# Attention gradients: accumulating dV and dK transposed, with 512-column moving operands and a crossbar turn of the result

## The chip, the cores and the metric

The kernel runs on one core of a Trainium2 chip. The metric is the device time of one execution in microseconds (us), the median of several. All runs quoted here were classed as fast runs: the granted TensorE clock was 0.994 to 0.998 of full speed in the profiled ones. Kernels are compared only within the same rounds. Engines are named PE (TensorE), PEld (its weight loads), DVE (VectorE), ACT (ScalarE), POOL (GpSimd) and SP (SyncE, which only issues DMAs here).

## The reference, cut to what matters

The reference computes a residual block (attention over a given K and V, times a gated MLP) and all its gradients. Only the attention and its gradients matter here; they take about 3.1 of the 5.0 ms. There are 32 heads, 2048 queries, 2048 keys and a head size of 128.

```python
q = (x @ wq).reshape(B, Sq, H, Dh)            # H = 32, Dh = 128, Sq = Sk = 2048
scores = einsum("bhqd,bhkd->bhqk", q, k_cache) * Dh ** -0.5
p = softmax(scores)
o = einsum("bhqk,bhkd->bhqd", p, v_cache)
# ... and by jax.vjp:   dV = P^T dO,   dP = dO V^T,   dS = P * (dP - delta),
#                       dK = dS^T Q,   dQ = dS K
```

## The kernel before: the parts that the change and the argument touch

A head takes 32 slots. In the first 16 ("pass 1") each slot makes one slab P of 128 queries x 2048 keys; in the next 16 ("pass 2") each turns one P slab into a dS slab in place. Each finished slab is turned by the DMA crossbar (issued by SP), and five slots later (`skew`) PE multiplies the turned slab (PT or dST) by V or K to get the output and dQ. PE's order is fixed in the program: if a turned slab has not landed by its slot, PE stands.

```python
            wpt = pool("wpt", 7 if fast else 4)      # turned slabs in flight
            skew = min(SKEW if fast else 2, NT // 2) # SKEW = 5
            def transpose_slab(hs, qt, name):
                T = wpt.tile([P, NT, P], bf, name=name, tag="PT")
                nc.sync.dma_start_transpose(T[:], hs.slabs[qt][:])   # 128 x 2048, 512 KB
                return T
            def tail_part(hs, T, rhs, part):         # uses the turned slab, L677
                ...
                for kt in range(part * NT // 2, (part + 1) * NT // 2):
                    nc.tensor.matmul(hs.acc[:, 0, :], lhsT=T[:, kt, :], rhs=rhs[:, kt, :], ...)
```

dV and dK are sums over the 16 slabs of a pass. They are taken in two halves of eight slabs (the first half is parked in SBUF as f32), a step of eight matmuls at a time, in between the rest. Before the change the *slab* is the stationary operand, so every 128x128 block of it is loaded as weights for one matmul of 128 columns:

```python
            class Partial:
                def step(self):
                    kt = self.kt
                    j = kt % 4
                    if j == 0:
                        self.tile = acc_tile()
                    for qt in range(self.lo, self.hi):
                        nc.tensor.matmul(self.tile[:, j, :], lhsT=self.slabs[qt][:, kt * P:(kt + 1) * P], rhs=self.rhs[:, qt, :], ...)   # L737
                    ...
                            fo_ = stg.tile([P, 4, P], bf, name="kvo", bufs=4)
                            nc.vector.scalar_tensor_tensor(fo_[...], self.tile[...], self.factor, self.part[...], ...)
                            nc.gpsimd.dma_start(self.out_dram...[:, k0:kt + 1, :], fo_[:, :j + 1, :])   # 128 KB
```

In the last head, SP also loads the first two blocks of the attention output, turned (`load_oT`, 1 MB each, into the buffers KQ and xnT), for the output projection that follows, and POOL loads rows of `wo`.

## Time and profile before

| | before |
|---|---|
| median (4 runs of the comparison) | 5018.9 us |
| attention, from the first dO^T matmul to the last head's | 3014.9 us, 31 heads |
| one head (distance of the heads' first dO^T matmuls) | 97.37 us, in 28 of 30 full heads to within 0.01 us |
| last head, to the first matmul of the output projection | 121.2 us |
| output projection | 148.4 us |
| all that follows | 1256.1 us |

The stretches are read from the starts of the first matmuls of each kind in the trace. These are lines of the page of the kernel before: busy time by engine, the digits of PE and its clock over 40 slices, DMA queues (packets, MB, share of 16 engines) and the costliest groups (busy us, mean ns of one, idle time before them).

```profile
PE 4914.6 (98%) x53584; PEld 3475.1 (69%) x54480; DVE 2582.2 (51%) x6721; ACT 2575.9 (51%) x4637; POOL 961.8 (19%) x1507
PE   9999999999999999999999999999889999999999
PEclk9999999999999999999999999999999999999999
...
q1 hardware_dynamic: 2659746, 699.38, 75.7%
q8 instruction: 428, 7.01, 0.6%
...
L737 PEld LDWEIGHTS <-Pq 128*128 128x128 bf16 x16384 | 1003.9, 98 | 244.3 <-issue 1.1
...
L737 PE MATMUL acc<-dOn,Pq 128*128 128x128 bf16 x8192 | 552.3, 219 | 10.1
L737 PE MATMUL acc<-Qn,Pq 128*128 128x128 bf16 x8192 | 540.6, 219 | 3.4
```

PE is the bound. A matmul's duration (219 ns) says little, because matmuls overlap; what counts is the distance of starts. The timeline of the kernel before shows it (start us, duration us, engine, line, operation, count):

```profile
1507.17 0.59 PE L700 MATMUL dp<-VT,dOT 128*128 128x512 bf16 x2
1507.60 1.06 PE L677 MATMUL acc<-Vn,PT 128*128 128x128 bf16 x16
1508.49 0.59 PE L700 MATMUL dp<-VT,dOT 128*128 128x512 bf16 x2
1508.92 1.06 PE L737 MATMUL acc<-dOn,Pq 128*128 128x128 bf16 x16
```

Two matmuls of 512 columns occupy 0.43 us (215 ns each) and sixteen of 128 columns 0.89 us (56 ns each): four narrow ones cost 224 ns where one wide one costs 216. The Trainium skill, page "TensorE: Matmul & The Clock Gate", section "Back-to-back issue gap", gives N/2.4 + 2.5 ns for N columns, and this trace agrees. The list of waits of PE in the 30 full heads has a single entry, so nothing else that the list shows delays PE there:

```profile
engine line waited for: us in total, times, longest us
PE acc L677 <- DMA dST<-Pq: 1.0, 1, 1.0
```

### The profile page before, as it was taken

To read this page: it belongs to the slowest core of one execution; us is meant where nothing else is said; L and a number is where in the kernel's file an instruction comes from. 1 tells how busy PE (TensorE), PEld (TensorE's weight loads), DVE (VectorE), ACT (ScalarE), POOL (GpSimd) and SP (SyncE) were. 2 spreads that over 40 slices of the span, in tenths; PEclk is the share of its full clock that TensorE was granted. 3 is DMA by queue.
4 is the path that set the end of the run, shared out by engine and by line. 5 is a ranking of instruction groups with operands and counts; after the bars stand their busy time and mean duration, and the time that the engine had idled before them with its cause. 6 is when DMAs were issued, how large, how long until landed. Compare 5 with 4: busy or idle time off the path is not lost.

```text
span 5024.2 us, 128236 instructions
## 1 busy us (share of the span) xinstructions
PE 4914.6 (98%) x53584; PEld 3475.1 (69%) x54480; DVE 2582.2 (51%) x6721; ACT 2575.9 (51%) x4637; POOL 961.8 (19%) x1507
## 2 busy tenths in 40 slices
PE   9999999999999999999999999999889999999999
PEld 4445787787787788778778877877646666555554
DVE  4545666666666666666666666665425444200111
ACT  5422766766666676666667666666413333211000
POOL 3322111111111111111111111111222222211000
PEclk9999999999999999999999999999999999999999
DMA  7887999999999999999999999999996665797876
GB/s 260 273 206 167 211 213 205 206 215 212 202 214 216 201 212 208 214 208 209 215 202 213 206 213 210 209 215 203 209 196 206 195 189 183 223 264 178 171 140 121
DMA packets 2762803, 1031.39 MB, mean 205 GB/s; under 512 B 2665377, under 2 KB 2669602, under 8 KB 2762210
## 3 DMA queue, kind: packets, MB, share of 16 engines
q1 hardware_dynamic: 2659746, 699.38, 75.7%
q0 software_dynamic: 101856, 323.05, 20.0%
q8 instruction: 428, 7.01, 0.6%
q14 instruction: 165, 1.35, 0.1%
q10 hardware_dynamic: 608, 0.59, 0.0%
HBM read 175.31 MB, written 182.13 MB: 71 GB/s over the span
## 4 chain that ended last, share of the span: by engine, by line
PE 92%; DMA 3%; issue 3%; DVE 1%; ACT 0%; SPq 0%; POOL 0%; POOLq 0%; ACTq 0%; DVEq 0%
PE acc L737 18%; PE acc L677 18%; PE acc L975 13%; PE sp L630 8%; PE dp L700 7%; PE acc L1157 6%; PE acc L213 6%; PE u_ps L448 3%; PE g_ps L446 3%; PE dh L1036 3%; PE acc L531 3%; PE acct L146 2%; PE acc L945 2%; DMA dST<-Pq 1%; DMA xnT<-on_d 1%
## 5 line engine op out<-in xcount | busy, mean ns | idle before, releaser
L648 ACT ACTIVATE Pq<-sp 128x1024 bf16<-128x1024 f32 x1024 | 1048.1, 1024 | 309.7 <-PE sp L630 196.4
L737 PEld LDWEIGHTS <-Pq 128*128 128x128 bf16 x16384 | 1003.9, 98 | 244.3 <-issue 1.1
L703 DVE SCALAR_TENSOR_TENSOR Pq<-dp,negdelta,Pq 128x1024 bf16<-128x1024 f32 x512 | 655.3, 1280 | 37.7 <-PE acc L677 36.5
L706 ACT ACTIVATE t<-dp,negdelta 128x1024 bf16<-128x1024 f32 x512 | 568.1, 1116 | 178.4 <-PE dp L700 123.0
L677 PEld LDWEIGHTS <-PT 128*128 128x128 bf16 x8192 | 501.0, 98 | 128.6 <-DMA PT<-Pq 11.5
L677 PE MATMUL acc<-Vn,PT 128*128 128x128 bf16 x8192 | 547.4, 219 | 17.0 <-DMA PT<-Pq 10.1
L737 PE MATMUL acc<-dOn,Pq 128*128 128x128 bf16 x8192 | 552.3, 219 | 10.1
L677 PE MATMUL acc<-Kn,dST 128*128 128x128 bf16 x8192 | 551.3, 219 | 9.1 <-DMA dST<-Pq 5.5
L630 PE MATMUL sp<-KQ 128*128 128x512 bf16 x1762 | 547.1, 379 | 2.2 <-ACT Pq L648 2.1
L737 PE MATMUL acc<-Qn,Pq 128*128 128x128 bf16 x8192 | 540.6, 219 | 3.4
L700 PE MATMUL dp<-VT,dOT 128*128 128x512 bf16 x1728 | 540.8, 379 | 0.0
L707 DVE TENSOR_TENSOR Pq<-t,Pq 128x1024 bf16<-128x1024 bf16 x512 | 354.6, 693 | 359.7 <-ACT t L706 351.9
L677 PEld LDWEIGHTS <-dST 128*128 128x128 bf16 x8192 | 492.0, 98 | 68.2 <-DMA dST<-Pq 7.4
L718 ACT ACTIVATE dq_n<-acc,rsc 128x128 bf16<-128x128 f32 x512 | 188.4, 368 | 331.7 <-PE acc L677 329.4
L1174 DVE SCALAR_TENSOR_TENSOR junk<-acc,xn_all 128x512 f32<-128x512 f32 (+1 forms) x32 | 13.9, 453 | 635.6 <-ACT dxn L1173 635.6
L751 POOL DMA_DIRECT2D out_dram<-kvo x256 | 140.8, 550 | 999.7 <-DVE kvo L749 999.7
L671 POOL DMA_DIRECT2D on_d<-o_n x128 | 97.3, 760 | 721.4 <-DVE junk L689 374.8
L1038 DVE TENSOR_TENSOR du_blk<-dh,ah 128x256 bf16<-128x256 f32 x288 | 120.4, 419 | 195.5 <-PE dh L1036 193.4
L1173 ACT ACTIVATE dxn<-acc 128x512 f32<-128x512 f32 (+1 forms) x32 | 12.8, 407 | 396.7 <-PE acc L1157 389.2
L635 DVE TENSOR_REDUCE rs_all<-rsp 128x1 f32<-128x2 f32 x512 | 78.1, 153 | 255.7 <-ACT Pq L648 253.4
L50 DVE TENSOR_SCALAR o_n<-acc,rinv_all 128x128 bf16<-128x128 f32 x352 | 123.3, 350 | 161.5 <-PE acc L677 161.5
L648 ACT ACTIVATION_READ_ACCUMULATOR Pq<-sp 128x1 f32 x1024 | 200.5, 196 | 0.0
(213 smaller groups left out, 6977.0 us busy)
## 6 DMA issues: line engine op xcount, KB each, us to landing
out_dram<-kvo POOLq DMA_DIRECT2D x256, 128.0 KB, 4.2
ah<-a_d POOLq DMA_DIRECT2D x18, 1024.0 KB, 7.2
ah<-h_d POOLq DMA_DIRECT2D x18, 1024.0 KB, 9.4
du_d<-du_blk POOLq DMA_DIRECT2D x18, 1024.0 KB, 8.0
dg_d<-dg_blk POOLq DMA_DIRECT2D x18, 1024.0 KB, 9.7
h_d<-h_row POOLq DMA_DIRECT2D x64, 256.0 KB, 3.5
a_d<-a_row POOLq DMA_DIRECT2D x64, 256.0 KB, 3.7
x_all<-in_A_k_cache_dram SPq DMA_DIRECT2D x64, 256.0 KB, 3.8
```

The costliest lines, as they stand in the source:

```text
L213: nc.tensor.matmul(av[:, :CH], lhsT=w[:, i, :], rhs=srcT[:, i, cs], start=(i == 0), stop=(i == DT - 1))
L630: nc.tensor.matmul(sp[:, c * CH:(c + 1) * CH], lhsT=hs.QT[:, qt * P:(qt + 1) * P], rhs=hs.KT[:, hf * HW_ + c * CH: hf * HW_ + (c + 1) * CH ...
L648: nc.scalar.activation(Pq[:, hsl], sp[:], AF.Exp, scale=SCALE, accum_out=hs.rsp[:, hf:hf + 1])
L677: nc.tensor.matmul(hs.acc[:, 0, :], lhsT=T[:, kt, :], rhs=rhs[:, kt, :], start=(kt == 0), stop=(kt == NT - 1))
L700: nc.tensor.matmul(dp[:, c * CH:(c + 1) * CH], lhsT=hs.dOT[:, qt * P:(qt + 1) * P], rhs=hs.VT[:, hf * HW_ + c * CH: hf * HW_ + (c + 1) * C ...
L703: nc.vector.scalar_tensor_tensor(Pq[:, hsl], dp[:], hs.negdelta[:, qt:qt + 1], Pq[:, hsl], op0=ALU.add, op1=ALU.mult)
L706: nc.scalar.activation(t[:], dp[:], AF.Identity, bias=hs.negdelta[:, qt:qt + 1], scale=1.0)
L707: nc.vector.tensor_tensor(Pq[:, hsl], t[:], Pq[:, hsl], op=ALU.mult)
L718: nc.scalar.activation(hs.dq_n[:, qt % G4, :], hs.acc[:, 0, :], AF.Copy, scale=hs.rsc[:, qt:qt + 1])
L737: nc.tensor.matmul(self.tile[:, j, :], lhsT=self.slabs[qt][:, kt * P:(kt + 1) * P], rhs=self.rhs[:, qt, :], start=(qt == self.lo), stop=(q ...
L975: nc.tensor.matmul(accs[j][:, :nn], lhsT=lhs[:, st, cols], rhs=rhs[:, st, n0:n0 + nn], start=(st == 0), stop=(st == NT - 1))
L1157: nc.tensor.matmul(self.accs[sl][j][:, :nn], lhsT=ch[:, kk, sl * P:(sl + 1) * P], rhs=wT[:, k0 + kk, n0:n0 + nn], start=(self.k + kk == 0) ...
```

## The change

The intent is to exchange the operands: dO and Q become the (few) stationary blocks, and the slabs are streamed as 512-column moving operands. The result is then dV^T and dK^T. It is collected in the K^T and V^T buffers, which are dead at that time, turned by the crossbar into a new tile and stored in one piece. The rebuilding of K^T and V^T for the next use is moved to later slots, to leave the buffers free for so long.

```diff
                 def step(self):
-                    for qt in range(self.lo, self.hi):
-                        nc.tensor.matmul(self.tile[:, j, :], lhsT=self.slabs[qt][:, kt * P:(kt + 1) * P], rhs=self.rhs[:, qt, :],
+                    chunk, j = divmod(self.n, SUB)                   # SUB = 4 steps per 512-column chunk
+                    cs = slice(chunk * CH, (chunk + 1) * CH)
+                    for qt in range(self.lo + m * j // SUB, self.lo + m * (j + 1) // SUB):
+                        nc.tensor.matmul(self.acc, lhsT=self.nat[:, qt, :], rhs=self.slabs[qt][:, cs],
                                          start=(qt == self.lo), stop=(qt == self.hi - 1))
                     ...
-                            fo_ = stg.tile([P, 4, P], bf, name="kvo", bufs=4)
-                            nc.vector.scalar_tensor_tensor(fo_[:, :j + 1, :], ...)
-                            nc.gpsimd.dma_start(self.out_dram...[:, k0:kt + 1, :], fo_[:, :j + 1, :])
+                    nc.vector.scalar_tensor_tensor(self.turned[:, cs], self.acc, self.factor, self.part[:, cs], ...)
+                    if chunk == NCH - 1:
+                        kvn = stg.tile([P, NT, P], bf, name="kvn", bufs=1)
+                        nc.sync.dma_start_transpose(kvn[:], self.turned)
+                        nc.gpsimd.dma_start(self.out_dram.rearrange("(p t) d -> p t d", t=NT), kvn[:])
...
-                    put(pl + q(skew + 3), NT * P, lambda: prep_kt(hd()))
+                    put(pl + q(NTH + 4), NT * P, lambda: prep_kt(hd()))
...
-                put(b1 + q(NSC + 2), NT * P, lambda: prep_vt(hd()))
+                put(b1 + q(NTH + 3), NT * P, lambda: prep_vt(hd()))
...
+                spread(b2, ... parts["v"], hd().KT, out_3[0, h], None))
+                spread(b2 + NT, ... parts["k"], VT[:], out_2[0, h], None, SCALE))
```

More of the change, by code (lines that the diff above doesn't have):

```diff
@@ L587 @@
     NSC = S // CH
+    SUB = NT // NCH
     nb = CH // P
@@ L721, in attention, with __init__ @@
             class Partial:
-                def __init__(self, hs, lo, hi, rhs, part, out_dram, eng, factor=1.0):
-                    self.factor = factor
-                    self.lo, self.hi, self.rhs = lo, hi, rhs
-                    self.part, self.out_dram, self.eng = part, out_dram, eng
-                    self.kt = 0
-                    self.tile = None
+                def __init__(self, hs, lo, hi, nat, part, turned, out_dram, eng, factor=1.0):
+                    self.lo, self.hi, self.nat, self.factor = lo, hi, nat, factor
+                    self.part = part[:].rearrange("p t d -> p (t d)")
+                    self.turned, self.out_dram, self.eng = turned, out_dram, eng
+                    self.n = 0
@@ L729, in __init__ @@
                     self.slabs = hs.slabs
                 def step(self):
-                    kt = self.kt
-                    j = kt % 4
+                    chunk, j = divmod(self.n, SUB)
+                    self.n += 1
+                    cs = slice(chunk * CH, (chunk + 1) * CH)
                     if j == 0:
-                        self.tile = acc_tile()
-                    for qt in range(self.lo, self.hi):
-                        nc.tensor.matmul(self.tile[:, j, :], lhsT=self.slabs[qt][:, kt * P:(kt + 1) * P], rhs=self.rhs[:, qt, :],
+                        self.acc = acc_tile()[:].rearrange("p a b -> p (a b)")[:, :CH]
@@ L738, in step @@
+                    m = self.hi - self.lo
+                    for qt in range(self.lo + m * j // SUB, self.lo + m * (j + 1) // SUB):
+                        nc.tensor.matmul(self.acc, lhsT=self.nat[:, qt, :], rhs=self.slabs[qt][:, cs],
                                          start=(qt == self.lo), stop=(qt == self.hi - 1))
-                    self.kt += 1
-                    if j == 3 or self.kt == NT:
-                        k0 = kt - j
-                        if self.out_dram is None:
-                            if self.factor == 1.0:
-                                alt.copy(self.part[:, k0:kt + 1, :], self.tile[:, :j + 1, :], eng=self.eng)
-                            else:
-                                alt.scaled(self.part[:, k0:kt + 1, :], self.tile[:, :j + 1, :], self.factor, eng=self.eng)
-                        else:
-                            fo_ = stg.tile([P, 4, P], bf, name="kvo", bufs=4)
-                            nc.vector.scalar_tensor_tensor(fo_[:, :j + 1, :], self.tile[:, :j + 1, :], self.factor, self.part[:, k0:kt + 1, :],
-                                                           op0=ALU.mult, op1=ALU.add)
-                            nc.gpsimd.dma_start(self.out_dram.rearrange("(p t) d -> p t d", t=NT)[:, k0:kt + 1, :], fo_[:, :j + 1, :])
@@ new lines, in step @@
+                    if j < SUB - 1:
+                        return
+                    if self.out_dram is None:
+                        if self.factor == 1.0:
+                            alt.copy(self.part[:, cs], self.acc, eng=self.eng)
+                        else:
+                            alt.scaled(self.part[:, cs], self.acc, self.factor, eng=self.eng)
+                        return
+                    nc.vector.scalar_tensor_tensor(self.turned[:, cs], self.acc, self.factor, self.part[:, cs], op0=ALU.mult, op1=ALU.add)
@@ L813, in first @@
                     parts[key] = part_tile()
-                    return Partial(hd(), lo, hi, rhs, parts[key], None, eng, factor)
+                    return Partial(hd(), lo, hi, rhs, parts[key], None, None, eng, factor)
                 spread(b1 + NTH, lambda: first("v", hd().dOn, 0, NTH, "v"))
-                spread(b2, lambda: Partial(hd(), NTH, NT, hd().dOn, parts["v"], out_3[0, h], None))
+                spread(b2, lambda: Partial(hd(), NTH, NT, hd().dOn, parts["v"], hd().KT, out_3[0, h], None))
                 spread(b2 + NTH, lambda: first("k", hd().Qn, 0, NTH, "s", SCALE))
-                spread(b2 + NT, lambda: Partial(hd(), NTH, NT, hd().Qn, parts["k"], out_2[0, h], None, SCALE))
+                spread(b2 + NT, lambda: Partial(hd(), NTH, NT, hd().Qn, parts["k"], VT[:], out_2[0, h], None, SCALE))
                 for qt in range(NT):
```

## The prediction

> **What bounds the kernel now.** TensorE, by issue. The page has PE busy 98% of 5024 us; the granted clock is 0.997. In the list of waits, all of PE's waits in the attention stage (about 480 to 3620 us) come to some 20 us, most of it in the last head. The attention repeats every 97.37 us per head (distance of the heads' first dO^T matmuls, equal in nearly all heads). From start to start, a 128-column matmul takes 55.9 ns and a 512-column one 215.8 ns (starts in the trace). A head has 168 of 512 columns and 1093 of 128: 36.25 + 61.10 = 97.35 us, which is the period. So PE never pauses, weight loads (98 ns each, groups) are hidden, and columns set the time. VectorE and ScalarE are busy 64% and 67% there (windows).
>
> The Trainium skill (TensorE: Matmul & The Clock Gate, "Back-to-back issue gap") gives N/2.4 + 2.5 ns, which this trace confirms (56 and 216 ns); its sustained figure of about 81 ns for weight load plus 128 columns is not what this trace shows (55.9).
>
> **What the change does.** dV and dK take 512 matmuls of 128 columns per head, each with its own weights; after it 128 of 512 columns. Columns are equal, so only the fixed part falls: 512 x 55.9 = 28.62 us become 128 x 215.8 = 27.62 us. That is 1.0 us per head, 32 us in all, all of it on the critical path because PE is dense.
> Drains stay 16 per head of 128x512, about 0.69 us on VectorE and 0.60 on ScalarE (groups). Four 128 KB stores per result become one of 512 KB.
> Added: two crossbar transposes per head beside 32. At the best rate in the trace (about 1136 packets of 256 B per us, 290 GB/s) one takes 1.85 us; issue takes SyncE about 2 us, more in bursts. Transposes' minimum goes from 59 to 63 us per head of 97, so bandwidth does not become the bound. They do join the queue of the probability and dS transposes. From landing to first use those have a median slack of 4 to 5 us in the middle of the first pass and 8 to 10 us around slots 10 to 12 of the second, with minima near 1 us. One transpose and the store behind it delay the next few by 2 to 4 us, at most sometimes a stall. I allow 3 us in all.
> K^T and V^T are rebuilt later (slots 12 and 11): same work, moved; the transposes will have read those buffers by then.
> After the last head, dK must be turned on SyncE before the third attention-output load, in a stretch which already waits on such loads (8.1 and 4.6 us in the timeline): I allow 4 us.
>
> **Predicted time.** 5019 - 32 + 3 + 4, about 4994 us (-0.5%). Range 4980 to 5014. Chances: faster by over 2%: 0.02; within 2%: 0.94; slower by over 2%: 0.04.
>
> **What the profile would show.** Weight loads of dV/dK fall from 16384 to 4096 and busy PEld by some 750 us, with no matching gain; head period near 96.4 us; starts of the new matmuls 216 ns apart; 1088 slab-sized transposes in place of 1024; PE waits for PT and dST a few us longer; first output-projection matmuls a few us later after attention.
>
> **What would make it wrong.** Transposes arriving late in every head (one stall of 1 us per head cancels the gain); K^T's or V^T's rebuild waiting on the turned result, which would halt ScalarE or VectorE and then PE; a hidden cost of weight loads that is larger than the start spacing shows.

## The result, and the profile after

The changed kernel took 5016.18 us (median of 4 runs, 5002.06 to 5021.0) against 5018.9 us (5015.51 to 5020.46). The ratio is 0.9991, with a 95% interval of 0.9970 to 1.0012. A ratio here is the mean time of one kernel's fast runs over the mean of the other's fast runs of the same rounds, so it is not quite the ratio of the medians. The predicted 4994 us was not reached, and 5016 us lies outside the range.

The lines of the page of the changed kernel that answer to those shown of before:

```profile
PE 4939.7 (98%) x42192; PEld 2960.8 (59%) x42192; DVE 2575.1 (51%) x6721; ACT 2573.5 (51%) x4637; POOL 854.4 (17%) x1315
PE   9999999999999999999999999999799999999999
PEclk9999999999999999999999999999999999999999
...
q1 hardware_dynamic: 2792866, 732.94, 76.5%
q8 instruction: 332, 5.44, 0.4%
...
L739 PE MATMUL acc<-Pq,dOn 128*128 128x512 bf16 x2048 | 531.4, 379 | 0.0
L739 PE MATMUL acc<-Pq,Qn 128*128 128x512 bf16 x2048 | 525.5, 379 | 0.0
...
L739 PEld LDWEIGHTS <-Qn 128*128 128x128 bf16 x2048 | 200.3, 98 | 240.7 <-issue 0.8
L739 PEld LDWEIGHTS <-dOn 128*128 128x128 bf16 x2048 | 199.0, 98 | 234.3 <-issue 0.8
```

The mechanism is there: a quarter of the weight loads, 512-column matmuls that start 216 ns apart (mean in the trace), and an undisturbed head of 96.46 us instead of 97.37 us, which is 0.91 us less, or 29 us over 32 heads. (PE's busy time is no measure of this: in the trace of before some matmul records are missing, 1762 of 2048 for one group.) But some heads are now longer: seven of the 30 full heads exceed 96.46 us by over 0.1 us, the worst is 100.91 us, and the excess sums to 13.9 us (before: 1.3 us above 97.37). The waits of PE in the full heads of the changed kernel (the list counts from the modelled end of a matmul, so its sum, 10.4 us, falls short of the 13.9):

```profile
PE acc L678 <- DMA dST<-Pq: 8.1, 7, 2.5
PE acc L678 <- DMA PT<-Pq: 2.3, 2, 1.9
```

What happens at such a place is seen in the timeline of the changed kernel (in brackets, idle time before it and what ended it):

```profile
842.34 2.94 SPq L752 DMA_TRANSPOSE kvn<-KQ  x1
845.37 16.98 SPq L625 DMA_TRANSPOSE dST<-Pq  x6
847.23 0.54 POOL L753 DMA_DIRECT2D out_dram<-kvn  x1 [6.60 <-DMA kvn<-KQ]
847.76 0.54 POOL L172 DMA_DIRECT2D wo_h<-in_A_wo_dram  x1
848.29 0.54 POOL L174 DMA_DIRECT2D wo_h<-in_A_wo_dram  x1
853.25 1.03 PE L739 MATMUL acc<-Pq,Qn 128*128 128x512 bf16 x4
856.74 1.46 PE L678 MATMUL acc<-Kn,dST 128*128 128x128 bf16 x16 [2.46 <-DMA dST<-Pq]
```

SP issues the turn of dV (`kvn<-KQ`), and the dS slabs behind it on the same in-order queue come later; POOL stands idle for 6.60 us, until the turn has landed, then issues the store and what had piled up behind it; a few slots later PE stands 2.46 us for a dS slab, that of slot 8, the second one behind the turn. Of the nine waits in the list above five, with 6.8 of the 10.4 us, are for the dS slab of slot 8 (counted in the trace by slab). That DMA waits are waited out by the issuing engine is also what the Trainium skill says (page "DMA: Bandwidth & Descriptors", section "Anatomy of one DMA — SWDGE (gpsimd) path": "DMA engines do not wait on semaphores"), and the 6.60 us in POOL's line, which issues the store, agree with it.

In the last head the waits grow as well. First the list of waits of before, then of the changed kernel, in that stretch:

```profile
PE acc L677 <- DMA PT<-Pq: 10.1, 2, 7.5
PE acc L677 <- DMA dST<-Pq: 3.4, 3, 1.6
PE acc L945 <- issue: 2.7, 2, 2.5
```

```profile
PE acc L678 <- DMA dST<-Pq: 12.6, 4, 10.0
PE acc L678 <- DMA PT<-Pq: 10.3, 1, 10.3
PE acc L947 <- DMA xn_all<-on_d: 0.9, 1, 0.9
```

Where the time went, by stretch of the profiled executions (`again` and `noturn` are experiments below: the changed kernel once more, and the changed kernel without the turn):

| us | before | changed | again | noturn |
|---|---|---|---|---|
| up to the first head | 483.6 | 483.5 | 483.5 | 483.4 |
| 31 heads | 3014.9 | 2998.2 | 3004.8 | 2985.8 |
| of it above 96.46 (before: 97.37) in 30 heads | 1.3 | 13.9 | 20.5 | 1.4 |
| last head | 121.2 | 127.5 | 128.1 | 119.2 |
| output projection | 148.4 | 143.9 | 149.0 | 138.8 |
| rest | 1256.1 | 1263.6 | 1255.6 | 1253.2 |
| span | 5024.2 | 5016.7 | 5021.1 | 4980.3 |

The matmuls gave 29 us. About 13 to 19 us of it went to stalls in full heads, and some 7 us to the last head (127.5 or 128.1 against 121.2 less 0.9). The 7.5 us more in the rest of the first profile are not the change's: `again` does not have them.

### The profile page after: what moved, and what is told of

Read it like the earlier page. It is cut to its first block, busy times and chain, and to the rows that moved or that the text cites. A ratio compares the mean times of both kernels' runs of the same rounds, so it can differ in the third digit from the quotient of the medians.

```text
span 5016.7 us, 104161 instructions
## 1 busy us (share of the span) xinstructions
PE 4939.7 (98%) x42192; PEld 2960.8 (59%) x42192; DVE 2575.1 (51%) x6721; ACT 2573.5 (51%) x4637; POOL 854.4 (17%) x1315
## 4 chain that ended last, share of the span: by engine, by line
PE 93%; DMA 4%; issue 2%; DVE 1%; ACT 0%; SPq 0%; POOL 0%; POOLq 0%; ACTq 0%; DVEq 0%
PE acc L678 18%; PE acc L739 17%; PE acc L977 13%; PE sp L631 9%; PE dp L701 9%; PE acc L1159 7%; PE acc L213 5%; PE u_ps L448 3%; PE g_ps L446 3%; PE dh L1038 3%; PE acc L531 3%; PE acct L146 2%; PE acc L947 2%; DMA dST<-Pq 1%; DMA PT<-Pq 1%
## 5 line engine op out<-in xcount | busy, mean ns | idle before, releaser
L704 DVE SCALAR_TENSOR_TENSOR Pq<-dp,negdelta,Pq 128x1024 bf16<-128x1024 f32 x512 | 654.9, 1279 | 38.6 <-PE dp L701 38.6
L678 PEld LDWEIGHTS <-dST 128*128 128x128 bf16 x8192 | 510.8, 98 | 174.2 <-DMA dST<-Pq 26.9
L631 PE MATMUL sp<-KQ 128*128 128x512 bf16 x2048 | 609.3, 379 | 2.2 <-ACT Pq L649 2.1
L701 PE MATMUL dp<-VT,dOT 128*128 128x512 bf16 x2048 | 609.8, 379 | 0.1
L678 PE MATMUL acc<-Kn,dST 128*128 128x128 bf16 x8192 | 562.6, 219 | 20.8 <-DMA dST<-Pq 20.8
L739 PE MATMUL acc<-Pq,dOn 128*128 128x512 bf16 x2048 | 531.4, 379 | 0.0
L739 PE MATMUL acc<-Pq,Qn 128*128 128x512 bf16 x2048 | 525.5, 379 | 0.0
L1176 DVE SCALAR_TENSOR_TENSOR junk<-acc,xn_all 128x512 f32<-128x512 f32 (+1 forms) x32 | 13.9, 453 | 643.0 <-ACT dxn L1175 643.0
L739 PEld LDWEIGHTS <-Qn 128*128 128x128 bf16 x2048 | 200.3, 98 | 240.7 <-issue 0.8
L739 PEld LDWEIGHTS <-dOn 128*128 128x128 bf16 x2048 | 199.0, 98 | 234.3 <-issue 0.8
L631 PEld LDWEIGHTS <-KQ 128*128 128x128 bf16 x2048 | 179.3, 98 | 124.2 <-issue 3.3
L701 PEld LDWEIGHTS <-dOT 128*128 128x128 bf16 x2048 | 177.7, 98 | 109.9 <-issue 1.0
## 6 DMA issues: line engine op xcount, KB each, us to landing
dg_d<-dg_blk POOLq DMA_DIRECT2D x18, 1024.0 KB, 10.3
```

Of the source, the lines that this page charges most:

```text
L631: nc.tensor.matmul(sp[:, c * CH:(c + 1) * CH], lhsT=hs.QT[:, qt * P:(qt + 1) * P], rhs=hs.KT[:, hf * HW_ + c * CH: hf * HW_ + (c + 1) * CH ...
L701: nc.tensor.matmul(dp[:, c * CH:(c + 1) * CH], lhsT=hs.dOT[:, qt * P:(qt + 1) * P], rhs=hs.VT[:, hf * HW_ + c * CH: hf * HW_ + (c + 1) * C ...
L704: nc.vector.scalar_tensor_tensor(Pq[:, hsl], dp[:], hs.negdelta[:, qt:qt + 1], Pq[:, hsl], op0=ALU.add, op1=ALU.mult)
L739: nc.tensor.matmul(self.acc, lhsT=self.nat[:, qt, :], rhs=self.slabs[qt][:, cs], start=(qt == self.lo), stop=(qt == self.hi - 1))
```

## The experiments

Theories at the start. TURN: the two added crossbar turns use up the time that slab turns have to spare. STORE: the single 512 KB store does it. MOVE: the later rebuilds of K^T and V^T do it. LUMP and QUEUE are two forms of TURN: one big piece at a bad moment, or the mere amount. All kernels gave the right result except `noturn`.

| run | median us | before, same batch | ratio | 95% interval | excess in 30 full heads, us |
|---|---|---|---|---|---|
| changed | 5016.2 | 5018.9 | 0.9991 | 0.9970 to 1.0012 | 13.9 |
| noturn (wrong result) | 4982.1 | 5019.8 | 0.9934 | 0.9920 to 0.9947 | 1.4 |
| twice | 5109.8 | 5019.8 | 1.0202 | 1.0181 to 1.0223 | 94.2 |
| moved | 5023.3 | 5019.8 | 1.0013 | 0.9999 to 1.0026 | 7.7 |
| chunk | 4999.4 | 5019.8 | 0.9961 | 0.9948 to 0.9975 | 6.3 |
| movedturn | 5079.4 | 5020.5 | 1.0118 | 1.0102 to 1.0133 | 39.4 |
| skew6 | 5008.4 | 5020.5 | 0.9966 | 0.9953 to 0.9980 | 6.9 (see below) |
| chunklate | 4998.9 | 5020.5 | 0.9958 | 0.9944 to 0.9971 | 5.2 |
| blate | 5015.4 | 5020.5 | 0.9991 | 0.9977 to 1.0004 | 1.4 |
| skew6paced | 4999.4 | 5019.6 | 0.9964 | 0.9952 to 0.9975 | 7.1 (see below) |
| chunkpaced | 4996.3 | 5019.6 | 0.9956 | 0.9943 to 0.9969 | 1.6 |
| bpaced | 5021.9 | 5019.6 | 1.0008 | 0.9995 to 1.0021 | 1.1 |
| chunkturn | 5040.2 | 5019.6 | 1.0033 | 1.0020 to 1.0046 | 37.9 |
| again (changed) | 5019.4 | 5025.2 | 0.9984 | 0.9967 to 1.0000 | 20.5 |
| s4now | 5021.8 | 5025.2 | 0.9996 | 0.9980 to 1.0011 | 14.9 |
| s4spaced | 5015.9 | 5025.2 | 0.9975 | 0.9961 to 0.9989 | 6.6 |
| s4spacedpaced | 4998.3 | 5025.2 | 0.9950 | 0.9934 to 0.9965 | 4.8 |
| wotied | 5018.4 | 5018.7 | 1.0002 | 0.9988 to 1.0016 | 10.3 |
| chunkturnwo | 5044.9 | 5018.7 | 1.0054 | 1.0041 to 1.0067 | 23.4 |

The excess is the sum of head periods above 96.46 us (97.37 us for the kernels that keep the old matmuls), from one profile each. It varies by some us from run to run, as `changed` and `again` show, and the profiled run is not always a typical one: that of `chunkturn` was its slowest (5060.9 us), that of `chunkturnwo` its fastest (5021.4 us), that of `s4spaced` its slowest (5025.1 us).

### noturn: the turn taken away

```diff
-                        nc.sync.dma_start_transpose(kvn[:], self.turned)
-                        nc.gpsimd.dma_start(self.out_dram.rearrange("(p t) d -> p t d", t=NT), kvn[:])
+                        nc.gpsimd.dma_start(self.out_dram.rearrange("(p t) d -> p t d", t=NT), self.turned.rearrange("p (t d) -> p t d", d=P))
```

> The changed kernel without the crossbar turn: dV^T and dK^T are stored as they lie, 512 KB at once (wrong result in these two outputs on purpose). Theory TURN (the two added transposes use up the slack): stalls in the full heads fall from 12 us to about 1 us as before the change, total 4990 to 4998 us. Rival STORE (the single 512 KB store starves the transposes, not the turn): stalls stay near 12 us, total about 5014 us.

4982.14 us, 0.9934: this is faster than expected and the whole gain that the matmuls promise, and a little more. In its profile the surplus lies after the attention: the output projection took 138.8 us instead of 148.4, with 8.1 us of waits instead of 16.8; why is open. The matmuls, the moved rebuilds and a single 512 KB store of each result are all still in it, so STORE and MOVE cannot be the cause by themselves. PE's waits in its full heads:

```profile
PE acc L678 <- DMA PT<-Pq: 0.8, 1, 0.8
PE acc L678 <- DVE rinv_all L637: 0.3, 1, 0.3
```

### twice: the turn doubled

```diff
                         nc.sync.dma_start_transpose(kvn[:], self.turned)
+                        nc.sync.dma_start_transpose(kvn[:], self.turned)
```

> The changed kernel with each result turned twice, the second time into the same buffer (right result): four added transposes per head in place of two. Theory TURN: the stalls grow by as much again or more, 25 to 60 us in all, total 5035 to 5070 us. Rival STORE: total within 5 us of the changed kernel.

5109.81 us, slower than TURN's own range. By the ratios, one turn per result costs 25 to 29 us (0.9984 or 0.9991 less 0.9934), the second 106 to 109 us more. The doubling is not clean, though: the second turn writes the same buffer, and in 27 of the 31 cases in which the landing of the first is recorded it starts within 0.06 us of that landing. SP's queue stood some 34 us for this in all 64 turns, and the rebuild of V^T waited too. So it is not shown that the cost of a turn grows with their number. The longest waits of PE between 576 and 3480 us of `twice`, nearly all of its full heads:

```profile
PE acc L678 <- DMA dST<-Pq: 37.4, 39, 3.0
PE acc L678 <- DMA PT<-Pq: 24.7, 30, 3.3
PE acc L739 <- DVE VT L42: 4.5, 3, 2.6
```

The traces of the three kernels show how. For each turned slab I took the time from its landing to its first use by PE, its slack (the landing is recorded for about half of the slabs or more; medians over 30 heads). The middle column is the changed kernel.

| slack, us | noturn | changed | twice | before |
|---|---|---|---|---|
| PT of slot 10 | 6.1 | 3.2 | 0.0 | 4.9 |
| PT of slot 12 | 5.4 | 3.3 | 1.5 | 4.7 |
| PT of slot 14 | 6.6 | 3.8 | 1.5 | 5.4 |
| dST of slot 10 | 8.2 | 5.6 | 0.9 | 7.8 |
| dST of slot 12 | 9.9 | 7.1 | 3.5 | 9.0 |
| dST of slot 14 | 11.5 | 10.1 | 5.3 | 11.6 |

Against `noturn`, a turn behind slot 7 takes 2 to 3 us from the slack of the slabs behind it, and not only of the next one or two: in pass 1 the delay is still there at slot 14 (2.8 us), in pass 2 it has shrunk to 1.4 us. The landings of slots 7 to 9, the first three behind the turn, are recorded neither in `noturn` nor in before; in the changed kernel the medians of slot 8 are 2.1 us (PT) and 3.6 us (dST), with minima of 0.0. SP had little free time to catch up: in the traces, between 1000 and 3000 us, SP's transposes were being issued during 75% of the time in `noturn`, 86% in the changed kernel and 92% in `twice` (80% before).

### moved: only the rebuilds moved

> The kernel before, with only the rebuilding of K^T and V^T moved to the later slots (12 and 11) as the change does. Theory TURN or LUMP: no matmul and no transfer changes, period 97.37 us, total within 4 us of before (5019). Rival MOVE (the later slots crowd the engines or the PSUM buffers and cause the stalls): stalls of 10 us or more, total above 5028 us.

The edit is the two `put` lines of K^T and V^T of the change, in the kernel before. The time was 5023.25 us, ratio 1.0013 with an interval that touches 1. So the later slots cost at most a few us (its one profile has 7.7 us of excess); with `noturn`, which has them too and no stall, MOVE falls as the main cause.

### movedturn: pointless turns in the old kernel

```diff
+                put(b2 + NTH - 1, 1, lambda: nc.sync.dma_start_transpose(KT.rearrange("p (t q) -> p t q", q=P), hd().Kn[:].rearrange("p t d -> p (t d)")))
+                put(b2 + NT + NTH - 1, 1, lambda: nc.sync.dma_start_transpose(VT[:]..., heads[h + 1].Kn[:]...))   # not in the last head
```

> The kernel before with the later rebuilds (as in the run moved, 5023 us) and two pointless crossbar turns per head at the moments of the change (K as it lies into the dead K^T and V^T buffers, never read; right result). The old matmuls stay. Theory TURN (a turn costs by itself, whatever the matmuls are): +25 to +45 us over moved, 5048 to 5070 us. Rival: the cost belongs to the change's other parts (its matmuls, the chain drain - turn - store), then within 8 us of moved.

5079.44 us, more than expected: by the ratios 53 us over `moved`. The turn costs by itself, with the old matmuls and with no store behind it. It costs more than in the changed kernel. These turns had nothing to wait for and were issued earlier, before the last slab of the pass before; behind them the slack of dST 3 and 4 fell from medians of 2.3 and 2.8 us before to 0.0 and 0.7 us, and most of PE's waits, 23 of 34, are for dST 1 to 3. This fits that the moment matters too.

### skew6: one more slot of slack

The turned results go into the dead buffers of V and K, and the 4 KB that this frees hold an eighth turned slab.

```diff
-    SKEW = 5
+    SKEW = 6
-            wpt = pool("wpt", 7 if fast else 4)
+            wpt = pool("wpt", 8 if fast else 4)
-                        kvn = stg.tile([P, NT, P], bf, name="kvn", bufs=1)
-                        nc.sync.dma_start_transpose(kvn[:], self.turned)
+                        nc.sync.dma_start_transpose(self.kvn[:], self.turned)      # Vn for dV, Kn for dK
...
-                        put(pl + q(skew + 3 + c), 0, lambda c=c: load_v(hd(), c, 4))
+                        put(pl + q(skew + 5 + c), 0, lambda c=c: load_v(hd(), c, 4))
```

> The changed kernel with more slack: the turned dV and dK go into the dead V and K buffers, and the freed 4 KB hold an eighth slab-transpose buffer, so that each transposed slab has six slots instead of five to arrive. Theory SLACK (the turn costs only because slab transposes then miss their slot): stalls in full heads fall from 12 us to under 3 us, total 4980 to 4995 us. Rival RATE (the crossbar has not the capacity for 34 turns per head): stalls stay, about 5010 us or more.

The mechanism was confirmed and the time was missed. All 30 full heads are 96.69 us long: not one stall, with the same 34 turns per head. (96.69 instead of 96.46 is the 6.9 us of the table. It sits in one place: 71 us into each of these heads a dP matmul starts 0.45 us after the dK matmul before it, instead of 0.22, just after VectorE's `Pq<-dp` at L704 has ended.) The list of PE's waits in these heads is empty. So the crossbar can carry 34 turns per head, and RATE falls; what is missing in the changed kernel is slack. (The run gives slabs a slot and a buffer more, and also moves the turned results and V's loads; these are not separated.) The total was still 5008.4 us: in the profile PE waited 21 us up to the start of the output projection and another 11 us some 27 us into it.

### chunk and chunkturn: the turn in four pieces

```diff
-                    if chunk == NCH - 1:
-                        kvn = stg.tile([P, NT, P], bf, name="kvn", bufs=1)
-                        nc.sync.dma_start_transpose(kvn[:], self.turned)
-                        nc.gpsimd.dma_start(self.out_dram.rearrange("(p t) d -> p t d", t=NT), kvn[:])
+                    kvn = stg.tile([P, SUB, P], bf, name="kvn", bufs=4)
+                    nc.sync.dma_start_transpose(kvn[:], self.turned[:, cs])
+                    nc.gpsimd.dma_start(self.out_dram...[:, chunk * SUB:(chunk + 1) * SUB, :], kvn[:])
```

> The changed kernel, but each finished 128x512 chunk of dV^T/dK^T is turned at once and stored in 128 KB pieces: the same crossbar bytes and the same stored bytes, spread over four moments per result. Theory LUMP (one 512 KB turn plus one 512 KB store in a row push the following slab transposes past their slack): stalls in the 31 full heads fall from 12 us to under 4 us and the time to about 5000 us (-0.4% against before). Rival QUEUE (it is the number of bytes through the crossbar that costs, wherever they lie): stalls stay near 12 us or grow, 5014 to 5022 us. The head period without stalls is 96.46 us in both.

4999.39 us: with the same bytes, spread, the loss in full heads is 6.3 us instead of 13.9. LUMP fits better, though its "under 4 us" was not reached, and QUEUE, in its strict form, is wrong. `chunkturn` also turns in four pieces (into one tile), but stores once:

> The changed kernel, turned chunk by chunk as in the run chunk, but stored once per result (512 KB) as in the change. Theory LUMP-TURN (it is the 512 KB turn in one piece that costs): time as chunk, 4995 to 5004 us. Rival LUMP-STORE (it is the single 512 KB store): time as the changed kernel, 5010 to 5020 us.

5040.21 us, slower than before the change and outside both expectations. In these runs turning in pieces paid only together with storing in pieces. In its trace the four transfers that wait behind the last turn on POOL's queue (the store, a dQ store, two `wo` loads) are issued within 2 us of each other, and a dS slab turn under them takes 8.2 us to land. `chunk` has such a bunch too, with a 128 KB store in it and dS turns of up to 8.4 us, so the bunch alone does not explain the difference.

### s4now, s4spaced: the store in four pieces, turned whole

```diff
-                        nc.gpsimd.dma_start(self.out_dram.rearrange("(p t) d -> p t d", t=NT), kvn[:])
+                        for c in range(NCH):                                # s4now
+                            ts = slice(c * SUB, (c + 1) * SUB)
+                            nc.gpsimd.dma_start(self.out_dram...[:, ts, :], kvn[:, ts, :])
```

In `s4spaced` each piece is tied to a slab of slot 8, 10, 12 or 14 (POOL adds zero times an element of the slab to one element of `kvn`), so that it is issued from slots 9, 11, 13 and 15.

> The changed kernel itself once more, in the rounds of the next three: 5010 to 5020 us if nothing depends on the chip or the day; its full heads have 10 to 20 us of stalls.

> The changed kernel, one whole turn per result, the store cut into four of 128 KB (1 KB per row) issued one behind the other. Theory STORE-SIZE (the long rows of a 512 KB store are served before the crossbar's 256 B packets and hold them up): 12 to 20 us faster than the changed kernel, about 5000 us. Rival STORE-MOMENT (the bytes come at the wrong moment, right behind the turn): within 5 us of the changed kernel.

> As s4now, but the four stores are tied to dS and P slabs of the slots 9, 11, 13 and 15, so that they lie two slots apart. STORE-MOMENT: stalls in full heads fall under 3 us, total 4985 to 4997 us, at least as good as chunk (4999 us), which turns in four pieces. STORE-SIZE: as s4now.

`again` confirms the changed kernel (5019.41 us, 0.9984). `s4now` is no better than it, at 0.9996: the size of the stores is not the cause. `s4spaced` has fewer stalls in full heads (6.6 us), but only 0.9975 in time: its last head and its output projection were longer in the profile (134.7 and 155.4 us). The expected 4985 to 4997 us were missed.

### wotied, chunkturnwo: the loads behind the store moved away

```diff
-                    put(pl + q(4), 0, lambda: load_wo(hd()))
+                    put(pl + q(11), 0, wo_tied)     # first copies an element of dS slab 10 into wo_h
-                    put(pl + q(skew + 4), DT * P, lambda: prep_wot(hd()))
+                    put(pl + q(14), DT * P, lambda: prep_wot(hd()))
```

> The changed kernel with the two loads of the next head's wo tied to dS slab 10 (slot 11 instead of right behind the 512 KB store), its transposes two slots later. Theory BUNCH (the store waits for the turn at the head of GpSimd's in-order queue, and what piles up behind it, the dQ store and these loads, then runs together with it and holds up the slab transposes): stalls in full heads fall from about 17 us (after 13.9, again 20.5) to under 8 us, total 5 to 12 us below the changed kernel. Rival: no change, within 4 us.

> The run chunkturn (ratio 1.0033 to before; 37.9 us of stalls in full heads) with the same tie. BUNCH: stalls in full heads fall below 22 us and the ratio below 1.000. Rival (the four turns on SyncE's queue themselves): within 5 us of chunkturn, ratio 1.002 or more.

Neither gained: 1.0002 and 1.0054. The pile behind the store, plausible as it looks in the timeline, is not what costs, at least not its `wo` part. The stalls of `wotied` (10.3 us) missed BUNCH's "under 8", those of `chunkturnwo` its "below 22" (23.4 us, in its fastest run). BUNCH finds no support. Why `chunkturn` is so much worse than `chunk` stays open.

### The last head: chunklate, blate, skew6paced, chunkpaced, bpaced, s4spacedpaced

The two 1 MB turning loads of the attention output were put among the slab turns of the last head on SP's queue by the order in which the program was scheduled. In the changed kernel one of them (into KQ) even stands behind the turn of dV, whose buffer it overwrites, and the slab turn behind it was issued over 7 us late. `chunklate` and `blate` issue both loads after the attention:

```diff
-            for st in range(min(2, NT)):
-                put(bl + NT + skew * st, 0, lambda st=st: load_oT(oTs[st], st))
...
-            if NT > 2:
-                load_oT(oTs[2], 2)
+            for st in range(min(3, NT)):
+                load_oT(oTs[st], st)
```

> The run chunk (4999 us) with the first two loads of the attention output for the output projection issued after the attention instead of within the last head. Theory LASTHEAD (these two 1 MB transposing loads stand before slab transposes in the last head and cost PE about 25 us of waits there): waits in the last head fall below 8 us, a new wait of about 7 us appears at the start of the output projection, total 4983 to 4994 us. Rival: the waits only move, total within 4 us of chunk.

> The kernel before with the same two loads moved behind the attention: the control for chunklate. PE waits 16 us in its last head, so theory LASTHEAD says 3 to 10 us faster than before, 5009 to 5016 us; rival: within 3 us.

For `chunklate` the rival was right: the waits for slab turns in the last head fell from 25 to 11 us, but the projection then started with a wait of 15.1 us for its first load, where I had expected 7. `chunklate` is as fast as `chunk`; `blate` is at 0.9991 (5015.4 us), which lies in LASTHEAD's range but is not clear of the noise. The `paced` kernels tie the loads to dS slabs 13 and 15 of the last head instead:

```diff
+            def paced_oT(st):
+                nc.gpsimd.tensor_copy(oTs[st][0:1, 0, 0:1], heads[H - 1].slabs[NT - 3 + 2 * st][0:1, 0:1])
+                load_oT(oTs[st], st)
-                put(bl + NT + skew * st, 0, lambda st=st: load_oT(oTs[st], st))
+                put(bl + NT - 2 + 2 * st, 0, lambda st=st: paced_oT(st))
```

> The run skew6 (5008 us; its 30 full heads are all 96.69 us long, without a stall, and its loss is in the last head and the start of the output projection), with the two first attention-output loads tied by a one-element copy to dS slabs 13 and 15 of the last head, so that they can not be issued ahead of most slab transposes. Theory LASTHEAD (these loads in front of slab transposes are what the last head waits for): waits in the last head fall from about 21 us to under 10 us, the output projection does not start with a wait over 8 us, total 4988 to 5000 us. Rival: wo loads and not these are the cause, or the waits move; total within 4 us of skew6.

> The run chunk (4999 us) with the same tie. LASTHEAD: last-head waits from 25 us to under 12 us, total 4984 to 4993 us. Rival: within 4 us of chunk.

> The kernel before with the same tie, as the control. LASTHEAD: its last-head waits fall from 16 us to under 8 us and the total to 5006 to 5014 us; so the changed kernel's own gain would be the distance of skew6paced and chunkpaced from this one, about 18 to 24 us of the 29 us that the matmuls save. Rival: within 4 us of before.

> s4spaced with the tied first loads of the attention output (as in skew6paced and chunkpaced, which gained 9 and 3 us by it, while the kernel before gained nothing): 3 to 9 us faster than s4spaced, and the best of all right kernels, 4980 to 4993 us.

The kernel before gained nothing from it (1.0008). Only `skew6paced` came within its expected total; `chunkpaced` and `s4spacedpaced` stayed 3 and 5 us above theirs. `skew6` went from 5008.4 to 4999.4 us, though in ratio only from 0.9966 to 0.9964, which are the same within their intervals; `chunk` from 0.9961 to 0.9956, also within them. `s4spaced` went from 0.9975 to 0.9950 in the same rounds (15 us between the means of five runs each, 95% interval 6 to 24), the one clear gain. PE's waits in the last head of `chunkpaced`:

```profile
PE acc L678 <- DMA dST<-Pq: 12.3, 6, 4.4
PE acc L951 <- issue: 3.5, 1, 3.5
PE acc L678 <- DMA PT<-Pq: 3.0, 1, 3.0
```

The 10 us waits are gone, but 15 us in shorter ones stay. The traces of the other runs divide these waits in part. PE's waits for slab turns in the last head, one profile each, are 4.7 us with neither added turns nor output loads there (`blate`), 13.4 us with the output loads alone (before and `noturn`), 10.7 us with turns in pieces alone (`chunklate`), 22.9 us with both (changed) and 24.7 us with both and turns in pieces (`chunk`). So turn and output loads both delay slab turns there; the `wo` loads are in all of these.

**A version that beats both.** `s4spacedpaced` (4998.29 us, 0.9950 of before; the changed kernel in the same rounds had 5019.41 us and 0.9984) and `chunkpaced` (4996.34 us, 0.9956) keep about 22 to 25 us of the 29 us. This is under half a per cent, and by the 2% measure still "the same".

## Why the prediction was wrong

- *"What bounds the kernel now. TensorE, by issue"*: right. The period of 97.37 us was the sum of the start distances, and without the turn the 31 heads took 29.1 us less.
- *"That is 1.0 us per head, 32 us in all"*: right within a tenth: 0.91 us and 29 us. The starts are 216 ns apart, as read before.
- *"Weight loads of dV/dK fall from 16384 to 4096 and busy PEld by some 750 us, with no matching gain"*: nothing in the runs contradicts it. The fall of PEld's busy time was 514 us, not the 750 us that I gave, since the group itself fell by 605 us, from 1003.9 to 399.3, and the weight loads of other matmuls rose by some 90 us.
- *"Transposes' minimum goes from 59 to 63 us per head of 97, so bandwidth does not become the bound"*: right as far as it goes. `skew6` carries 34 turns per head without a stall. But I then used the best rate, 1.85 us per turn, as if it were the load. With all other traffic SP's issue of transposes took 77 us per head before and 83 us after (of 97.4 and 96.5), and in a queue so full a delay goes away slowly.
- *"One transpose and the store behind it delay the next few by 2 to 4 us, at most sometimes a stall. I allow 3 us in all"*: **this is the step that failed.** The delay per turn was right (mostly 2 to 3 us of slack). Its consequence was mis-sized: the stalls of the full heads were 13.9 and 20.5 us in two profiles instead of 3. The slack that I set against the delay, 8 to 10 us in pass 2, was that of slots 10 to 12, further behind the turn; most of the waiting (6.8 of 10.4 us) is for the second slab behind it, dST 8, whose landing the trace of before does not record. The minima near 1 us that I had seen at other slots were a warning: with a delay of 2 to 4 us, in 32 heads and two passes each, the sum of the stalls had to be worked out and not waved through. I also took it that only "the next few" slabs suffer; in pass 1 the slack is still short at slot 14.
- *"After the last head ... I allow 4 us"*: mis-sized and misplaced. The last head lost some 7 us, and within it, not after it: two waits of about 10 us on slab turns, and one of the output loads now stood behind the turn of dV. `noturn` (119.2 us against 127.5) shows that this goes with the turn.
- *"K^T's or V^T's rebuild waiting on the turned result"*, named as a risk, was not seen in the changed kernel. It appears in `twice` (`PE acc L739 <- DVE VT L42`, 4.5 us).

Shown: the added crossbar turns are the cause (taken away, doubled, and added to the old kernel), and in the full heads they act by the slack of the slab turns (`skew6`). Open: why four turned pieces need four stores, what part the `wo` loads have in the last head's waits, and why the output projection of `noturn` waits less.

## What to carry to other kernels

A gain on a dense engine that was worked out from start distances came true here to a tenth; what pays for it has to be set against the slack of the very transfers that stand next behind it, by its minimum over all rounds and not its median, and against how full their in-order queue already is. Doubling a suspected cost is a cheap test, if the second copy brings no wait of its own, as it did in `twice`. If an added transfer must share a queue with transfers that the bound engine waits for, give those one slot more, or cut the added one in pieces along with the store behind it, and measure, since half of that measure (`chunkturn`) made things worse.

## What the Trainium skill lacked or had wrong

- "TensorE: Matmul & The Clock Gate", "Back-to-back issue gap": its figures for a sustained stream of weight loads and matmuls (about 81 ns for 128 columns, about 131 ns for 512) are not what these traces show, 55.9 and 216 ns with a weight load for each matmul. The formula that it calls isolated held in the dense stream.
- "Advanced Engine Details and Errata", "X-Bar Transpose (TRN2)": it expects 350 to 400 GB/s. The best that any microsecond of these traces between 1000 and 3000 us shows is 1136 packets of 256 B, 291 GB/s, and a 512 KB slab took 3.6 us at best and about 5 us in the median from issue to landing. Other transfers ran at the same time, so this is what a busy kernel got and not the limit of the crossbar.
- No page that I read tells that the crossbar's packets thin out while instructions are fetched. While a 16 KB packet of the instruction queue was in flight (about 1.0 us), the transposes moved 327 packets per us instead of 721 (before; 345 instead of 753 after). This is a coincidence in time in the traces, which no run varied on purpose. The change lowers the number of such packets from 428 to 332 as it has fewer instructions, a side effect that I had not thought of and that may be part of why `noturn` beat its expectation; no run separates it.
